# RWKV-7 recurrence and low-rank mixer on one core: 64-row products gathered, scans of 65, two raw buffers and a new order

## The chip, the cores and the metric

The kernel runs on one core of one Trainium2 chip. The metric is the device time in microseconds, the median of several runs. A profile of one further execution shows where the time goes: it has a span, from the first to the last instruction, and the execution's own time, which is a little longer.

The engines have short names: PE is TensorE (matrix products; PEld its weight loads), DVE is VectorE, ACT is ScalarE, POOL is GpSimd and SP is SyncE, which here only issues DMAs. Each engine works off its own queue in order.

## The reference

Two blocks follow each other. The first is a recurrence over 768 steps, for 4 batches and 8 heads of 40 channels. The second mixes along the sequence at rank 32 and then applies two projections with a ReLU between them.

```python
# r, k, v, w, a, b: (4, 8, 768, 40)
for t in range(S):
    y[:, :, t] = einsum('bhd,bhde->bhe', r_t, state)
    Sa = einsum('bhde,bhe->bhd', state, a_t)
    state = state * w_t[:, :, None, :] - einsum('bhd,bhe->bhde', Sa, b_t) \
            + einsum('bhd,bhe->bhde', v_t, k_t)
x = y.transpose(0, 2, 1, 3).reshape(4, 768, 320)
h = x.transpose(0, 2, 1) @ U @ V               # U (768, 32), V (32, 768)
u = x + h.transpose(0, 2, 1)
out = u + maximum(u @ w_ch1, 0) @ w_ch2        # w_ch1 (320, 1280), w_ch2 (1280, 320)
```

All inputs are made from random numbers; the six of the recurrence are float32, and the mixer's weights are 64-bit floating-point numbers in DRAM, which the kernel turns into float32 itself.

## The kernel before

**Units.** The sequence is cut into 12 chunks of 64 steps, and the batches into two pairs. A unit is one chunk of one batch pair, so there are 24 units; units 0 to 11 belong to the first pair and 12 to 23 to the second. Within a chunk the recurrence is written as products with a triangular matrix that has to be inverted; between chunks the state is carried.

**What a unit does.** Three functions write a unit's operations. `prep_f` (line 663) loads w, a, b and k, turns w over on TensorE (`wT`), and builds running products of w in both directions with two scans on VectorE: `bs` (line 686) runs backward over w in PSUM, `fs` (line 700) forward over a copy of w in SBUF that ScalarE makes (`WF`). Five blocks of 64 columns lie side by side; a one in `C1` and a zero in w at each block's border start a new product (`z`). `pl` and `rc` make the product over the whole chunk and its reciprocal. `Pn` turns the forward result over, `Q` the backward one; `KB` and `AH` (line 729) multiply k, b and a by them; the product `F` and its mask `mF` (line 789) give the triangular matrix, which goes to DRAM (`nd`) and comes back in lanes (`ln`).

`lanes` (line 794) inverts 32 x 32 triangles lane by lane, in thirty steps of two instructions each (lines 817 and 818), for all units of a group at once. Group 0 runs on VectorE, the others on POOL. Groups 0 and 1 (`F16`) take half as many steps and end with products on TensorE (`doubled`: `Ma`, `Mb`). The result goes through DRAM again (`gd`, `AB`). `prep_t` (line 845) makes the 64 x 64 inverse from the 32 x 32 ones (`XB` at line 871, then the products `T1` and `T2`). `carry` (line 904) is the serial part: `He`, `H`, `X` and `S` update the state, and `C` and `Y` give the unit's rows of y, which line 989 writes to `XTM`.

**The mixer.** `mixer` (line 1104) runs once for each batch pair, when its 12 units are done. `ph` is the product with U, `rs` adds partial sums, `V` is the product with V, and line 1140 adds it to x. Then follow six groups of two units. In each, u is turned over (`uT`, in three pieces of 128, 128 and 64 channels), ten blocks of 128 columns of w_ch1 give the hidden layer (`up`), ScalarE and VectorE apply the ReLU in turn (`hid`), and ten products per unit with w_ch2 give the result (`dn`). With 320 channels, each up block is two products on 128 rows and one on 64. Before, two blocks share a pair of PSUM banks, and the two 64-row products of the pair come last:

```python
def f(j=j, p=p):
    for y in range(2):
        mm(p.ap[:, y, 0:GN], W1[2][half(y), (j + y) * 128:(j + y + 1) * 128], ufs[2].ap[half(y)], start=False)
```

The third piece of u is needed in both halves of the partitions. Before, four ordinary products with an identity write it there.

**Weights.** `piece` (line 1031) loads a block of a weight into the raw buffer `CV` and converts it with two instructions on ScalarE and six on VectorE, with `CG` as scratch. There is one buffer of each. `weights1` brings w_ch1, U and V early, `weights2` brings w_ch2, in ten pieces.

**The order.** No line of the program says what comes when. Each operation is handed to a plan with an engine, an assumed duration, the buffers that it reads and writes, and a priority. `order` (line 185) then places them one by one: whichever engine is free takes the ready operation with the lowest priority number, if PSUM has room (three pairs of banks and two single ones). The base priority comes from the unit's number. To it is added an offset by the operation's name from the table `SHIFT` (line 1286), which has variants for early units (`0`) and those of the second pair (`*`). Where TensorE would fall idle for long, the plan puts in fillers (`idle`, line 1281): products of 512 columns in bfloat16 whose result is not read. The plan ends as a fixed order for each engine, and that order is what is compiled.

Of the kernel before, what the change touches and what calls it, by code (L numbers as in the profile page):

```python
# [53 lines left out]
class Op:  # L54
    __slots__ = ("eng", "ns", "fn", "pri", "deps", "users", "wait", "ps", "first", "mode", "start", "end", "lat",
                 "n", "left", "name", "ready", "act", "hw", "late")
# [9 lines left out]
class Pace:  # L66
# [8 lines left out]
    def worked(self, a, z, x):  # L75
        for i, w in enumerate(self.w):
            s = i * WIN / 2
            b, y, end = a + s, x, z + s
            while b < end - 1e-6:
                k = int(b // WIN + 1e-9)  # L80
                q = min(end, (k + 1) * WIN)
                if q <= b:
                    q = end
                part = y * (q - b) / (end - b)
                w[k] = w.get(k, 0.0) + part
                y -= part
                b = q
# [234 lines left out]


# [3 lines left out]
def kernel(  # L327
# [26 lines left out]
    NS = 5 * L  # L354
# [66 lines left out]
    nc.vector.memset(C1[:, L - 1:NS:L], 1.0)  # L421
# [49 lines left out]
    tRB, tQD = ring("tRB", 1, NS), ring("tQD", 1, 2 * NS)  # L471
    tFW, tD1, tWF = (ring(key, n, NS) for key, n in (("tFW", 1), ("tD1", 1), ("tWF", 1)))
# [17 lines left out]
    CG = ring("CG", 1, WP)  # L490
# [58 lines left out]
    for t in tWF:  # L549
        zeros([whole(t)], [t[:]], 320, -90.0)  # L550
# [17 lines left out]
    for t in tLT2:  # L568
        PL.add("DVE", 1700, lambda t=t: parts(t), w=[whole(t)], pri=-40.0, name="parts")
# [9 lines left out]
    PL.add("DVE", 1400, m16, w=[bM16], pri=-40.0, name="m16")  # L579
# [5 lines left out]
    GROUPS = [[0], [1, 2], [3, 4, 5], [6, 7, 8], [9, 10, 11], [12, 13, 14], [15, 16, 17], [18, 19], [20, 21], [22, 23]]  # L585
# [77 lines left out]
    def prep_f(n, pri, lane):  # L663
# [3 lines left out]
        RB, FW, D1, WF = B(tRB, n), B(tFW, n), B(tD1, n), B(tWF, n)  # L667
# [3 lines left out]
        def f():  # L671
            for x in range(2):
                tr(strided(pw.ap, [[128, 2], [1, L]], 64 * x), W.ap[:, 160 * x:160 * x + 128])
            for x in range(2):
                for y in range(2):
                    mm(pw.ap[64 * y + 32 * x:64 * y + 32 * x + 32, 256:320], W.ap[half(y), 160 * x + 128:160 * x + 160],
# [5 lines left out]
        PL.add("ACT", 435, lambda: act(WF.ap.rearrange("p (k t) -> p k t", t=L)[:, :, 1:],  # L682
                                       pw.ap[:, 0:NS].rearrange("p (k t) -> p k t", t=L)[:, :, 0:L - 1]),
               r=[pw], w=[WF], pri=pri, name=f"WF{n}")
        PL.add("DVE", 70, lambda: nc.vector.memset(pw.ap[:, 0:NS + 1:L], 0.0), r=[pw], w=[pw], pri=pri, name=f"z{n}")
# [8 lines left out]
                                       RB.ap.rearrange("p (c t) -> p c t", t=L).unsqueeze(2).to_broadcast([128, 5, 2, L])),  # L694
               r=[RB], w=[QD], pri=pri, name=f"dup{n}")
        PL.add("DVE", 175, lambda: nc.vector.tensor_tensor(out=w0.ap, in0=RB.ap[:, 0:NS:L], in1=WF.ap[:, 1:NS:L], op=ALU.mult),
               r=[RB, WF], w=[w0], pri=pri, name=f"pl{n}")
        PL.add("DVE", 190, lambda: nc.vector.reciprocal(out=D1.ap[:, 0:NS:L], in_=w0.ap),
               r=[w0], w=[D1], pri=pri, name=f"rc{n}")
        PL.add("DVE", 830, lambda: nc.vector.tensor_tensor_scan(  # L700
            out=FW.ap, data0=WF.ap, data1=D1.ap, initial=0.0,
            op0=ALU.mult, op1=ALU.add), r=[WF, D1], w=[FW], pri=pri, name=f"fs{n}")

        def f():
            for y in range(2):
                tr(pp.ap[:, y, 0:128], FW.ap[:, 128 * y:128 * y + 128])
            for y, x in QUADS:
                mm(pp.ap[half(x), y, 128:160], FW.ap[half(y), 256:320], ID[half(y), 64 * y + 32 * x:64 * y + 32 * x + 32])
        PL.add("PE", 617, f, r=[FW], w=[pp], pri=pri, mode=2, name=f"Pn{n}")
# [7 lines left out]
        def f():  # L717
# [3 lines left out]
            for x in range(2):  # L721
                for y, z in QUADS:
                    mm(pq.ap[half(z), y, 160 * x + 128:160 * x + 160], RB.ap[half(y), 256:320],
                       ID[half(y), 64 * y + 32 * x:64 * y + 32 * x + 32])
        PL.add("PE", 952, f, r=[QD, RB], w=[pq], pri=pri, mode=0, name=f"Q{n}")
        PL.add("DVE", 810, lambda: nc.vector.tensor_tensor(
            out=strided(S["KB"].ap, [[L, 2], [2 * L, NH], [1, D]]), in0=pq.ap[:, :, 0:DM].rearrange("p t (c e) -> p t c e", e=D),
            in1=KB.ap.rearrange("p (t c e) -> p t c e", t=2, e=D), op=ALU.mult), r=[pq, KB], w=[S["KB"]], pri=pri, name=f"KB{n}")
        PL.add("DVE", 500, lambda: nc.vector.tensor_tensor(
# [58 lines left out]
    def masked(o, p, m, pri, name):  # L788
        PL.add("DVE", 1200, lambda: nc.vector.tensor_tensor(  # L789
# [4 lines left out]
    def lanes(g, pri):  # L794
# [6 lines left out]
        eng, e = (nc.vector, "DVE") if g == 0 else (nc.gpsimd, "POOL")  # L801
# [9 lines left out]
        for j in range(1, top - 1):  # L811
# [7 lines left out]
            c = 450 + 3.3 * nd_ * j * m if e == "POOL" else 350 + 2.0 * nd_ * j * m  # L819
# [5 lines left out]
    def doubled(n, S, AB, DT, XB, pri):  # L825
# [10 lines left out]
        PL.add("DVE", 610, lambda p=p: nc.vector.tensor_tensor(  # L836
# [4 lines left out]
        PL.add("DVE", 610, lambda p=p: nc.vector.tensor_tensor(out=XB.ap, in0=p.ap, in1=AB.ap, op=ALU.add),  # L841
# [3 lines left out]
    def prep_t(n, lane, pri):  # L845
# [16 lines left out]
        else:  # L862
            for y in range(2):
# [7 lines left out]
            PL.add("DVE", 620, lambda: nc.vector.tensor_tensor(  # L871
                out=XB.ap.rearrange("p (h x t) -> p h x t", x=2, t=32),
                in0=AB.ap.rearrange("p (h t) -> p h t", t=32).unsqueeze(2).to_broadcast([128, NH, 2, 32]),
                in1=HB[:].unsqueeze(1).unsqueeze(3).to_broadcast([128, NH, 2, 32]), op=ALU.mult), r=[AB, bHB], w=[XB], pri=pri + 0.02,
                name=f"XB{n}")
# [28 lines left out]
    def carry(n, pri):  # L904
# [56 lines left out]
        if n + 2 < N:  # L961

            for u in range(2):
                PL.add("DVE", 380, lambda u=u: nc.vector.memset(
# [3 lines left out]
        PL.add("DVE", 1200, lambda: nc.vector.tensor_tensor(  # L968
# [27 lines left out]
    def decayed(n, pri):  # L996
# [12 lines left out]
        PL.add("DVE", 830, lambda: nc.vector.tensor_tensor(  # L1009
# [3 lines left out]
        PL.add("DVE", 500, lambda: nc.vector.tensor_tensor(  # L1013
# [17 lines left out]
    def piece(dst, dbuf, srcs, pri):  # L1031
# [7 lines left out]
        raw, g = B(CV, i), B(CG, i)  # L1039
        rb = raw.ap[:, 0:2 * n]  # L1040
# [484 lines left out]
```

## Time and profile before

| | |
|---|---|
| median of 3 runs | 765.96 us (764.36 to 768.99) |
| profiled execution, its own time | 766.89 us |
| its span | 765.1 us |
| mean granted TensorE clock | 0.956 |
| TensorE busy | 716.4 us (94%) |
| VectorE busy | 383.0 us (50%) |
| ScalarE busy | 274.4 us (36%) |
| GpSimd busy | 286.5 us (37%) |
| fillers (line 1283) | 272, busy 75.9 us |
| bytes moved by DMA | 53.51 MB, 97% of the packets under 512 B |

Busy time of an engine is the time in which one of its instructions runs. Products on TensorE are pipelined: the duration of one runs on while the next has begun, so costs are read from start to start. A float32 product shows as two records. The granted clock is 1 at full speed and 0.5 at half.

### The profile page before, as it was taken

What the parts mean: (1) busy time and instruction counts of PE and PEld (TensorE: products, weight loads), DVE (VectorE), ACT (ScalarE), POOL (GpSimd) and SP (SyncE); (2) the same over time, 40 slices, a digit from 0 to 9 for tenths busy, and PEclk for the clock granted to TensorE, in tenths of its full rate; (3) what the DMA queues carried; (4) which work ended last, traced back from release to release, by engine and by line L of the source; (5) the groups of instructions that cost most, each with busy time, mean ns of one, the idle gap of its engine ahead of it and who ended that gap; (6) DMA issues with size and microseconds to landing.
All of it is one profiled execution on the core that took longest, in us unless ns stands there. A gap on an engine that the chain in (4) does not pass through costs nothing.

```text
span 765.1 us, 27488 instructions
## 1 busy us (share of the span) xinstructions
PE 716.4 (94%) x12098; PEld 514.9 (67%) x12098; DVE 383.0 (50%) x743; ACT 274.4 (36%) x569; POOL 286.5 (37%) x551
## 2 busy tenths in 40 slices
PE   7998988897799997999989999999999999999997
PEld 4556767676677862676757777777877566767664
DVE  7685878785967777556740266641513311011110
ACT  3534545554545651154620264542432010111100
POOL 5004388965930048200087286588810000000000
PEclk8998989998889998999989999999999999999999
DMA  8766865655356462234640335521210000000001
GB/s 128 130 108 131 151 112 108 123 105 101 63 106 103 94 120 68 71 70 84 117 82 10 73 52 93 90 52 38 37 39 10 18 1 18 9 17 15 14 9 30
DMA packets 238111, 53.51 MB, mean 70 GB/s; under 512 B 230944, under 2 KB 234144, under 8 KB 237984
## 3 DMA queue, kind: packets, MB, share of 16 engines
q1 hardware_dynamic: 212640, 47.74, 33.1%
q10 hardware_dynamic: 25344, 3.94, 3.2%
q8 instruction: 97, 1.59, 0.8%
q14 instruction: 30, 0.25, 0.1%
HBM read 38.27 MB, written 13.37 MB: 68 GB/s over the span
## 4 chain that ended last, share of the span: by engine, by line
PE 67%; POOL 8%; DVE 8%; DMA 8%; ACT 4%; issue 4%; SPq 1%; ACTq 0%; DVEq 0%; POOLq 0%
PE pb L612 28%; PE pc L612 25%; PE pb L609 7%; PE pb L1283 5%; POOL tLN L818 4%; POOL tTM L817 4%; DMA tW<-in_w_dram 3%; PE pc L609 1%; DMA CV<-in_moe_w_ch_dram 1%; DMA tKB<-in_b_dram 1%; DMA tLN<-nd 1%; DMA tAB<-gd 1%; SPq L602 1%; ACT slot L605 1%; DMA tA<-in_a_dram 1%
## 5 line engine op out<-in xcount | busy, mean ns | idle before, releaser
L817 POOL TENSOR_TENSOR tTM<-tLN 64x108 f32<-64x108 f32 (+32 forms) x224 | 116.6, 520 | 205.7 <-DMA tLN<-nd 140.6
L612 PE MATMUL pb<-MX,W 128*128 128x256 f32 x720 | 160.2, 403 | 1.8 <-ACT slot L605 1.8
L612 PE MATMUL pc<-W,MX 128*128 128x320 f32 x440 | 134.2, 446 | 0.0
L612 PEld LDWEIGHTS pb<-MX,W 128*128 128x128 f32 x720 | 106.6, 189 | 38.6 <-issue 19.3
L818 POOL TENSOR_TENSOR tLN<-tLN,tTM 64x108 f32<-64x108 f32 (+32 forms) x224 | 123.6, 552 | 17.6
L612 PEld LDWEIGHTS pc<-W,MX 128*128 128x128 f32 x440 | 78.9, 189 | 39.2 <-issue 12.5
L605 ACT ACTIVATE MX<-pb 128x512 f32<-128x512 f32 (+3 forms) x45 | 25.3, 565 | 182.3 <-PE pb L612 182.2
L1283 PE MATMUL pb<-C,IDP 128*128 128x512 bf16 x262 | 72.7, 402 | 5.7 <-DVE slot L789 2.1
L1182 DVE TENSOR_SCALAR MX<-pb 128x512 f32<-128x512 f32 x24 | 16.5, 689 | 97.5 <-PE pb L612 97.5
L605 ACT ACTIVATE slot<-pb 128x160 f32<-128x160 f32 (+1 forms) x84 | 35.4, 448 | 38.2 <-PE pb L612 24.2
L1283 PEld LDWEIGHTS <-IDP 128*128 128x128 bf16 x272 | 24.0, 100 | 37.0 <-issue 16.4
L1197 DVE TENSOR_TENSOR MX<-pc,XTM 128x320 f32<-128x320 f32 x22 | 10.8, 491 | 71.6 <-PE pc L612 71.0
L968 DVE TENSOR_TENSOR tCG<-pb,MU 128x1024 f32<-128x1024 f32 x24 | 29.2, 1217 | 10.1 <-PE pb L612 9.4
L605 ACT ACTIVATE JK<-tW,WLO 128x320 bf16<-128x320 f32 x24 | 13.4, 560 | 49.4 <-DMA tW<-in_w_dram 47.1
L612 PE MATMUL pb<-tRT,tVXT 64*64 64x64 f32 x1536 | 29.9, 231 | 1.1 <-ACT tRT L605 1.0
L789 DVE TENSOR_TENSOR slot<-pb,MM 128x1024 f32<-128x1024 f32 x21 | 25.6, 1221 | 10.2 <-PE pb L612 10.1
L605 ACT ACTIVATE tVXT<-pb 128x1024 f32<-128x1024 f32 x24 | 24.6, 1024 | 15.8 <-PE pb L609 14.9
L605 ACT ACTIVATE tSB<-pb 64x320 f32<-64x320 f32 x44 | 19.0, 431 | 30.6 <-PE pb L609 24.8
L871 DVE TENSOR_TENSOR tXB<-tAB,HB 128x512 f32<-128x512 f32 x21 | 16.1, 767 | 26.8 <-DMA tAB<-gd 16.4
L612 PEld LDWEIGHTS pb<-tRT,tVXT 64*64 64x64 f32 x1536 | 26.6, 144 | 4.2 <-ACT tRT L605 1.2
L605 ACT ACTIVATE tKBT<-pb 128x1024 f32<-128x1024 f32 x24 | 24.5, 1021 | 11.6 <-PE pb L609 8.5
L612 PEld LDWEIGHTS pb<-slot,tKBT 64*64 64x64 f32 x1344 | 22.0, 135 | 9.8 <-issue 4.9
(241 smaller groups left out, 1143.0 us busy)
## 6 DMA issues: line engine op xcount, KB each, us to landing
CV<-in_moe_w_ch_dram SPq DMA_DIRECT2D x18, 320.0 KB, 3.4
nd<-slot SPq DMA_DIRECT2D x42, 128.0 KB, 2.8
tW<-in_w_dram SPq DMA_DIRECT2D x48, 80.0 KB, 3.7
tKB<-in_k_dram SPq DMA_DIRECT2D x48, 80.0 KB, 3.7
tR<-in_r_dram SPq DMA_DIRECT2D x48, 80.0 KB, 2.9
tVX<-in_v_dram SPq DMA_DIRECT2D x48, 80.0 KB, 3.3
out_dram<-MX SPq DMA_DIRECT2D x48, 80.0 KB, 2.1
tLN<-nd SPq DMA_DIRECT2D x21, 128.0 KB, 3.3
```

The source lines that it names most:

```text
L602: (eng or nc.sync).dma_start(out=o, in_=i)
L605: nc.scalar.activation(out=o, in_=i, func=kw.pop("func", ACTF.Copy), **kw)
L609: nc.tensor.matmul(out=o, lhsT=i, rhs=ident, is_transpose=True, start=True, stop=True, skip_group_check=True)
L612: nc.tensor.matmul(out=o, lhsT=l, rhs=x, start=start, stop=stop, skip_group_check=True)
L789: PL.add("DVE", 1200, lambda: nc.vector.tensor_tensor(out=o.ap.rearrange("p (s i t) -> p s i t", s=2, t=L), in0=p.ap[:].rearrange("p s (i ...
L817: eng.tensor_tensor(out=y, in0=at([[32, j], [0, m]], j), in1=at([[0, j], [1, m]], 33 * j + 1), op=ALU.mult)
L818: eng.tensor_tensor(out=at([[32, j], [1, m]], j + 1), in0=at([[32, j], [1, m]], j + 1), in1=y, op=ALU.add)
L871: PL.add("DVE", 620, lambda: nc.vector.tensor_tensor(out=XB.ap.rearrange("p (h x t) -> p h x t", x=2, t=32), in0=AB.ap.rearrange("p (h t) ...
L968: PL.add("DVE", 1200, lambda: nc.vector.tensor_tensor(out=CG.ap.rearrange("p (s t) -> p s t", t=L), in0=pc.ap[:].rearrange("p s (i t) -> p ...
L1182: PL.add("DVE", 680, lambda o3=o3, p=p: nc.vector.tensor_scalar_max(o3, p.ap[:, :, 0:GN], 0.0), r=[p], w=[hb], pri=q + 0.02, name=f"hid{pr}")
L1197: PL.add("DVE", 490, lambda p=p, n=n, ob=ob: nc.vector.tensor_tensor(out=ob.ap, in0=p.ap[:, 0:DM], in1=XTM[:, n, :], op=ALU.add), r=[p, xt ...
L1283: nc.tensor.matmul(out=t[:] if len(t.shape) == 2 else t[:, 0, :], lhsT=ib[:, 0:128], rhs=cb[:, 0:512], start=True, stop=True, skip_group_c ...
```

## The change

The parts of the change are these.

1. **64-row products of the up projection.** Four blocks now share a pair of PSUM banks, so ten blocks take three pairs. The 64-row products come first and together: in the first mixer the four, four and two of each pair of banks, in the second all ten in a row. The 128-row products follow. An eviction of the hidden layer covers two pairs of blocks instead of one.
2. **Third piece of u.** Two transposes write it to the lower half of the partitions, and two copies on VectorE bring it to both halves of SBUF. The other two pieces are both copied by ScalarE.
3. **Scans of 65.** A block is now 65 columns wide, with a border column before each 64. The zero of the backward scan and the start of the forward scan both lie there, so that both scans read w in PSUM. The copy `WF` and the product `pl` go; a small copy takes `pl`'s name. `Pn` becomes four products of 64 columns instead of two transposes.
4. **Groups and engines.** Units 0 and 1 are groups of their own, followed by groups of two to three; there are eleven groups instead of ten, and the short form `F16` covers two units instead of three. Group 0's lanes move to POOL, `AH` of units 0 to 5 moves to POOL, and `XB` moves to ScalarE as two instructions.
5. **Two raw buffers.** Weights alternate between `CV` and a part of W2's storage, until the pieces that lie there come up themselves; `CG` gets a second buffer.
6. **The order.** A base priority comes from the longest way from an operation to the end, with assumed durations and latencies. New offsets are added, with a class of its own for the units of group 2. The assumed durations of many operations are changed, and a rounding in the count of TensorE's activity is corrected.

```diff
+    def rank(self):
+        for o in self.ops[::-1]:
+            o.way = o.ns + GAP[o.eng] + max(((o.lat if u.eng != o.eng or o.eng == "SP" else 0.0) + u.way for u in o.users), default=0.0)
+            o.pri = -o.way / 15000.0
...
-    NS = 5 * L
+    NS = 5 * (L + 1)
...
-    CG = ring("CG", 1, WP)
+    CG = ring("CG", 2, WP)
...
-    GROUPS = [[0], [1, 2], [3, 4, 5], [6, 7, 8], [9, 10, 11], [12, 13, 14], [15, 16, 17], [18, 19], [20, 21], [22, 23]]
+    GROUPS = [[0], [1], [2, 3], [4, 5, 6], [7, 8, 9], [10, 11, 12], [13, 14, 15], [16, 17], [18, 19], [20, 21], [22, 23]]
+    AHP, LANV, XBA, ZXA = 6, 0, 1, 0
+    TAILS = ((0, 1, 2),)
...
-        PL.add("ACT", 435, lambda: act(WF.ap.rearrange("p (k t) -> p k t", t=L)[:, :, 1:],
-                                       pw.ap[:, 0:NS].rearrange("p (k t) -> p k t", t=L)[:, :, 0:L - 1]),
-               r=[pw], w=[WF], pri=pri, name=f"WF{n}")
...
-            out=FW.ap, data0=WF.ap, data1=D1.ap, initial=0.0,
-            op0=ALU.mult, op1=ALU.add), r=[WF, D1], w=[FW], pri=pri, name=f"fs{n}")
+            out=FW.ap, data0=pw.ap[:, 0:NS], data1=D1.ap, initial=0.0,
+            op0=ALU.mult, op1=ALU.add), r=[pw, D1], w=[FW], pri=pri, name=f"fs{n}")
...
-                tr(pp.ap[:, y, 0:128], FW.ap[:, 128 * y:128 * y + 128])
+                for x in range(2):
+                    mm(pp.ap[half(x), y, 0:128], FW.ap[:, G * (2 * y + x):G * (2 * y + x) + L], ID)
...
+        eng, e = (nc.gpsimd, "POOL") if n < AHP else (nc.vector, "DVE")
...
-        eng, e = (nc.vector, "DVE") if g == 0 else (nc.gpsimd, "POOL")
+        eng, e = (nc.vector, "DVE") if g < LANV else (nc.gpsimd, "POOL")
...
+                    PL.add("ACT", 390, lambda x=x: act(XB.ap.rearrange("p (h x t) -> p h x t", x=2, t=32)[:, :, x, :],
+                                                       AB.ap.rearrange("p (h t) -> p h t", t=32), scale=HB[:, x:x + 1]),
...
-        raw, g = B(CV, i), B(CG, i)
+        raw, g = PL.buf(W2F, 8 * DM, 8 * DM + 2 * WP) if i % 2 and dbuf not in bW2[8:] else B(CV, 0), B(CG, i)
...
+            for ks in (((0,), (1,), (2,)) if pr == 0 else TAILS):
+                js = [j for k in ks for j in quads[k]]
+                def f(js=js, dst=dst):
+                    for j in js:
+                        mm(dst(j), W1[2][half(j % 2), j * 128:(j + 1) * 128], ufs[2].ap[half(j % 2)], start=j % 4 < 2, stop=False)
...
+    PL.rank()
     for o in PL.ops:
         o.pri += SHIFT.get(kind(o.name) + o.late, 0.0)
```

## The prediction

> **What bounds the kernel now.** I read the page first, then the busy time by stage, then TensorE's order of time in the tail.
>
> ```profile
> span 765.1 us, 27488 instructions
> PE 716.4 (94%) x12098; PEld 514.9 (67%) x12098; DVE 383.0 (50%) x743; ACT 274.4 (36%) x569; POOL 286.5 (37%) x551
> PE   7998988897799997999989999999999999999997
> PEclk8998989998889998999989999999999999999999
> ```
>
> TensorE (PE) is the bound by share, but 94% is not all work: the kernel issues fillers, products of 512 columns whose result nobody reads (line 1283). So I cut the span where TensorE starts the two U products that open the two mixers (284.8 and 602.4 us by the rows of U) and asked for busy time by stage, first of everything, then of line 1283 alone (count in brackets).
>
> ```profile
> core 0: us, PE busy (x) PEld busy (x) DVE busy (x) ACT busy (x) POOL busy (x), PEclk, DMA share, GB/s
> 0.00:86.00 86.00, 74.49 (x1440) 48.52 (x1440) 61.20 (x159) 38.37 (x82) 21.44 (x63) 0.90 0.73 126
> 86.00:284.00 198.00, 174.65 (x4650) 137.35 (x4648) 148.24 (x270) 107.18 (x229) 110.83 (x200) 0.92 0.57 106
> 284.00:602.00 318.00, 309.33 (x5228) 222.30 (x5228) 149.28 (x269) 112.82 (x229) 154.22 (x289) 0.97 0.31 61
> 602.00:766.00 164.00, 157.94 (x792) 106.72 (x790) 24.28 (x47) 16.07 (x31) 0.00 (x0) 0.99 0.06 14
> ...
> 0.00:86.00 86.00, 25.05 (x94) 8.25 (x94) 0.90 0.73 126
> 86.00:284.00 198.00, 29.54 (x104) 8.63 (x104) 0.92 0.57 106
> 284.00:602.00 318.00, 17.31 (x58) 5.65 (x58) 0.97 0.31 61
> ```
>
> Stage 1 (to 284 us, the first twelve units) is held by waits: 34.9 us idle, 198 fillers, a granted clock of 0.90 to 0.92. Stage 2 (to 602 us, twelve units beside the first mixer) is TensorE's work, but for 8.7 us idle and 58 fillers. Stage 3, the second mixer alone, is TensorE without a gap, in six equal groups: the down products of one start at 675.11 and of the next at 699.69, so 24.58 us each. One group, TensorE in order of time (start, duration; a product of float32 has two records):
>
> ```profile
> 674.52 0.66 PE L612 MATMUL pc<-IDP,XTM 128*64 128x128 f32 x8
> 675.11 6.73 PE L612 MATMUL pc<-W,MX 128*128 128x320 f32 x24
> 681.67 2.52 PE L612 MATMUL pb<-MX,W 128*128 128x256 f32 x12
> 684.13 1.34 PE L612 MATMUL pc<-W,MX 128*128 128x320 f32 x4
> 685.31 2.52 PE L612 MATMUL pb<-MX,W 128*128 128x256 f32 x12
> ...
> 696.21 1.03 PE L612 MATMUL pb<-MX,W 128*128 128x256 f32 x4
> 697.07 0.38 PE L609 MATMUL pc<-IDP,XTM 128*128 128x128 f32 x2
> 697.29 1.03 PE L612 MATMUL pb<-MX,W 128*128 128x256 f32 x4
> ```
>
> Count from start to start, since durations overlap. Two full up products: 696.21 to 697.07, 0.43 us each. Twelve down products: 675.11 to 681.67, 0.547 each.
>
> **The gathered 64-row products.** The x12 row holds four full up products and one pair of 64-row ones: 681.67 to 684.13 is 2.46, less 4 x 0.43 leaves 0.74 for the pair. The two down products behind take 1.18 (684.13 to 685.31) where 2 x 0.547 is 1.09. A pair runs at once in the two halves of the rows, so its own work is 0.43; the other 0.31 + 0.09 = **0.40 us is the price of going to 64 rows and back**. A group has five pairs. The Trainium skill, "TensorEngine Tiling (Array Packing)", Key Properties, says that changing the tiling mode drains the array; that rule gives five pairs in a row one entry and exit. By row and rule a group saves 4 x 0.40 = 1.6 us; if instead each pass of 64 rows pays (no row shows two pairs together), it saves some 0.75. I take 1.6, because the U product, also on 64 rows, has 48 records from its start at 284.84 to that of the next product at 286.62: six passes of eight tiles and 320 columns, 0.30 each, where a down product's pass of 320 columns takes 0.27. Its entry and exit are paid once. The second mixer gathers all ten: 6 x 1.6 = 9.6. The first gathers 4, 4 and 2, three entries for five: 6 x 0.8 = 4.8. The gathered products hold all three pairs of PSUM banks at once; in the tail the last quad's eviction has 20 down products (10.9 us) to finish in, so I cost it at nothing.
>
> **The third transpose of u.** 674.52 to 675.11, 0.59 us for four plain products; now two transposes with 64 columns out. Two of 128 columns take 0.22 (697.07 to 697.29). The same skill page, Restrictions, speaks against it: column tiling disables transpose mode for float32, which would leave the 0.59. The gain is 0 to 0.37; I take 0.3, 12 times: 1.8 in each mixer. The second VectorE copy (0.42 us) hides behind down products.
>
> **The scans.** Line 700 takes 889 ns from SBUF, line 686 823 ns from PSUM; ScalarE loses WF (24 x 0.43), and the two pieces that replace pl stay near 0.2. The step of 65 costs TensorE: Pn's two transposes (about 0.31 to 0.37) become four 64-column products, by the row at 674.52 0.59. So +0.25, 24 times: 4.3 in stage 1, 1.8 in stage 2. pw stays in PSUM until the forward scan; the two single banks are also those of H, X, S and Y, which the new order must allow for.
>
> **Other engines.** Off VectorE in stage 1: XB (767 ns) of nine units, the three AH of units 3 to 5 and the three before them (0.6 each), the small lanes of group 0, and the doubling of unit 2: some 20 us of 209. On it: eight of the ten w_ch2 conversions now stand before the first U product (none did), some 3.2 us each. So VectorE is no lighter there, and much lighter in stage 2. POOL gains group 0's lanes, a thirty-step group of 64 rows (near 29 us) and six AH, in a stage where it was busy 132 of 284.
>
> **The order.** Every queue is reordered, so I go by what the instruction order shows. Fillers up to the first U product: 198 before, 244 after. From there to the second U product: 58 before, 5 after. Then: 16 before, 27 after. They mark where TensorE is expected to wait. Seventeen in a row at 292.28 last 3.84 us, 0.226 each; in half-clock stretches nearer 0.30.
>
> Stage 1: fillers +46 x 0.226 = +10.4; Pn +4.3; one unit less doubled -1.8; one PL group more +0.5; T1, T2 and X of one more unit already there +1.8; one wT and kT not yet -1.2. That is +14.0. Idle time was 34.9; unit 2 now waits for thirty lane steps, against which stand durations in the plan that are those of the rows (ST 640, was 500 for a row of 686; masked 1222, row 1217). I take -5.5, bounds -20 and +20. **+8.5**.
>
> Stage 2: 53 fillers less at 0.24, -12.7; gathering -4.8; transposes -1.8; Pn +1.8; units shifted -1.8 and +1.2; eight more down products of the first mixer left over, -4.3. Half the 8.7 us idle goes with the waits for w_ch2 and for u, -4.4.
>
> ```profile
> 298.00:309.00 11.00, 9.99 (x44) 0.53 0.19 60
> 387.00:394.00 7.00, 6.75 (x38) 0.53 0.59 92
> ```
>
> These two stretches (PE busy, then the clock) ran at near half clock: some 8.5 us lost. The Trainium skill, "TensorE: Matmul & The Clock Gate", says that an idle window of 3.4 us halves the clock; by it all 8.5 return where nothing idles, yet here PE was busy 91 to 96% in them. I take half, -4. **-30.8**; a new wait on w_ch2 or lanes would take the first term back.
>
> Stage 3: the eight down products +4.3; gathering -9.6; transposes -1.8; all V products now precede the first up products, each waiting for its VectorE addition (0.82), which the extra fillers mark, +2.5 for eleven. **-4.6**. A group becomes 24.58 - 1.6 - 0.3 = 22.7.
>
> Sum: -26.9 from the profiled execution's own 766.9 (its span 765.1 and 1.8 around it), **740**. The median of the runs shown is 766.0, 0.9 less, within what I can resolve; a measurement tells about 1%, so no change is 758.3 to 773.6.
>
> **Rivals.**
> - *The gain is smaller*: each 64-row pass pays (0.75 a group instead of 1.6, 0.3 instead of 0.8: 6 x 0.85 + 6 x 0.5 = +8), and half of the fillers removed from stage 2 come back as waits (+6): 754. For it: no row shows two pairs together. Against it: the U product.
> - *No change*: stage 1 lengthens by 34 instead of 8.5. For it: DMA share 0.73 at the start, K of two units is now issued ahead of the first W on SP (four issues, which took 3.76 us in the old order), and the new fillers stand in units 1, 2, 4 and 10. 765.
> - *Slower*: AH of units 3, 4 and 5 now stands in POOL's order among the lane steps of units 0 and 1. If its Pn or its A is late, the lanes behind it wait, then T1, X and every carry. Each costs up to a unit of stage 1, (284 - 86) / 11 = 18 us: 3 x 18 less the 8.5 counted, 785. It decides once the added waits pass 27 us. Against it: stage 1's POOL is idle more than half.
> - *The change does not do what it says*: the order lists four, two or ten 64-row products in a row, all scans of 65 and both raw buffers, so this gets no chance of its own.
>
> **Chances.** Forecast 0.62 (own range 726 to 755), smaller gain 0.20, no change 0.10, slower 0.08. Faster by over 1%: 0.82; within 1%: 0.10; slower: 0.08. The range runs from 718, where stage 1 sheds its bound of 20 and TensorE's whole half-clock loss of stage 2 returns, to 766, where the no-change rival ends; what is left out is the slower case and the edge of the others.
>
> **What would show it.** Right: six groups of 22.7 in the tail; the 64-row products in a row at about 0.22 a pass; fillers and idle nearly gone between the U products, which stand near 293 and 580; PEclk 9 from there on. Wrong: a group at 24 or more (gather), a first U product after 310 (stage 1, with POOL's waits for AH or tLN telling why), idle of over 10 us in stage 2.

## The result, and the profile after

The changed kernel took 742.92 us (median of 4 runs, 740.71 to 744.88); the kernel before took 765.16 us on the same chip (4 runs, 758.73 to 768.99). The ratio is **0.972, with a 95% interval of 0.964 to 0.979**: faster by 2.8%. The forecast was 740, so its sum holds to 3 us. Its stages hold less well, and most can be learned from them.

First the head of the page of the kernel after: span, busy time of the engines, and the two rows of 40 slices for TensorE and its granted clock.

```profile
span 741.5 us, 27587 instructions
PE 698.5 (94%) x12134; PEld 511.8 (69%) x12134; DVE 359.6 (49%) x688; ACT 280.2 (38%) x577; POOL 323.3 (44%) x645
PE   6889799898998898999999999999999999999997
PEclk9789999999999899999999999999999999999999
```

TensorE's share is the same 94%, now of a span that is 23.6 us shorter. VectorE has lost 23.4 us, ScalarE and POOL have gained 5.8 and 36.8. From the 17th slice on the row PE stands at 9 to the last slice but one, and the clock too; before, both rows still had an 8 in the 21st slice. So the share of busy time over the whole span does not show where the time went.

The two U products that open the mixers now start at 298.9 and 581.0 us. So the cut by stage is made at 299 and 581, and at 117, where the first rows of y are written. First everything, then the fillers alone (line 1313 now) in stage 1.

```profile
core 0: us, PE busy (x) PEld busy (x) DVE busy (x) ACT busy (x) POOL busy (x), PEclk, DMA share, GB/s
0.00:117.00 117.00, 98.51 (x1785) 62.49 (x1787) 81.99 (x185) 48.64 (x102) 69.49 (x162) 0.91 0.70 129
117.00:299.00 182.00, 165.08 (x4527) 126.18 (x4529) 132.19 (x252) 109.13 (x230) 97.37 (x179) 0.98 0.57 109
299.00:581.00 282.00, 280.15 (x5058) 210.34 (x5057) 119.56 (x207) 108.60 (x220) 156.43 (x305) 1.00 0.31 57
581.00:742.00 161.00, 154.78 (x782) 112.80 (x781) 25.90 (x48) 13.85 (x25) 0.00 (x0) 1.00 0.06 15
...
0.00:117.00 117.00, 37.99 (x125) 11.06 (x125) 0.91 0.70 129
117.00:299.00 182.00, 33.58 (x119) 9.44 (x119) 0.98 0.57 109
```

Read per stage, cut at the U products and at the ends of the span (idle time is the length of a stage less PE busy; the loss to the clock, used below, is a length times one less the granted clock):

| | stage 1 | stage 2 | stage 3 |
|---|---|---|---|
| length before, us | 284.8 | 317.6 | 162.7 |
| length after, us | 298.9 | 282.1 | 160.5 |
| difference | +14.1 | -35.5 | -2.2 |
| predicted | +8.5 | -30.8 | -4.6 |
| TensorE idle, before to after, us | 34.9 to 35.4 | 8.7 to 1.9 | 5.2 to 5.7 |
| fillers, before to after | 198 to 244 | 58 to 5 | 16 to 27 |

Stage 2 is where the time came from: TensorE has a 282 us stage with 1.9 us idle, five fillers (1.59 us busy) and a granted clock of 1.00.

In stage 3, one group in TensorE's order (start, duration, engine, line, form, count; a float32 product has two records):

```profile
629.00 0.38 PE L615 MATMUL pc<-IDP,XTM 128*64 128x128 f32 x2
629.21 1.89 PE L618 MATMUL pb<-MX,W 128*128 128x256 f32 x8
630.94 0.38 PE L615 MATMUL pc<-IDP,XTM 128*128 128x128 f32 x2
631.16 0.38 PE L615 MATMUL pb<-IDP,XTM 128*128 128x128 f32 x2
631.38 11.24 PE L618 MATMUL pc<-W,MX 128*128 128x320 f32 x40
642.55 9.53 PE L618 MATMUL pb<-MX,W 64*128 64x256 f32 x52
651.92 0.38 PE L615 MATMUL pc<-IDP,XTM 128*64 128x128 f32 x2
```

The third piece of u is the row at 629.00, two transposes, and the next row starts 0.21 us later (0.59 for four products before). The ten 64-row products stand first in the row at 642.55, with 32 records of 128 rows behind them; the pieces of u of one group and the next are 651.92 - 629.00 = **22.92 us** apart, as against 24.58 before and 22.7 predicted.

### The profile page after: what moved, and what is told of

The parts are those of the page before. It is cut to its first block, busy times and chain, and to the rows that moved or that the text cites. A ratio compares the mean times of both kernels' runs of the same rounds, so it can differ in the third digit from the quotient of the medians.

```text
span 741.5 us, 27587 instructions
## 1 busy us (share of the span) xinstructions
PE 698.5 (94%) x12134; PEld 511.8 (69%) x12134; DVE 359.6 (49%) x688; ACT 280.2 (38%) x577; POOL 323.3 (44%) x645
## 3 DMA queue, kind: packets, MB, share of 16 engines
q8 instruction: 97, 1.59, 0.9%
## 4 chain that ended last, share of the span: by engine, by line
PE 77%; DMA 9%; DVE 4%; ACT 4%; issue 3%; SPq 2%; ACTq 1%; POOL 0%; DVEq 0%; POOLq 0%
PE pb L618 40%; PE pc L618 23%; PE pb L615 8%; PE pb L1313 5%; DMA W<-in_moe_w_ch_dram 2%; SPq L608 2%; DMA CV<-in_moe_w_ch_dram 2%; PE pc L615 1%; DMA tVX<-in_v_dram 1%; DMA tW<-in_w_dram 1%; DMA tA<-in_a_dram 1%; DMA tAB<-gd 1%; DVE tCG L980 1%; DMA tR<-in_r_dram 1%; ACT slot L611 1%
## 5 line engine op out<-in xcount | busy, mean ns | idle before, releaser
L823 POOL TENSOR_TENSOR tTM<-tLN 64x84 f32<-64x84 f32 (+11 forms) x268 | 133.8, 499 | 140.8 <-DMA tLN<-nd 110.4
L824 POOL TENSOR_TENSOR tLN<-tLN,tTM 64x84 f32<-64x84 f32 (+11 forms) x268 | 139.0, 519 | 21.0
L618 PE MATMUL pb<-MX,W 64*128 64x256 f32 (+1 forms) x720 | 141.6, 388 | 0.0
L618 PEld LDWEIGHTS pb<-MX,W 64*128 64x128 f32 (+1 forms) x720 | 110.0, 188 | 29.2 <-issue 13.8
L618 PE MATMUL pc<-W,MX 128*128 128x320 f32 x400 | 124.5, 444 | 0.2
L611 ACT ACTIVATE MX<-pb 128x1024 f32<-128x1024 f32 (+4 forms) x37 | 24.7, 674 | 183.9 <-PE pb L618 182.9
L1210 DVE TENSOR_SCALAR MX<-pb 128x1024 f32<-128x1024 f32 x12 | 14.7, 1225 | 74.1 <-PE pb L618 74.1
L976 DVE MEMSET tVX<- 64x320 f32 x44 | 14.3, 325 | 34.6 <-PE pc L618 13.3
L618 PE MATMUL pb<-W,MX 128*128 128x320 f32 x80 | 29.9, 457 | 0.0
L876 DVE STREAM_TRANSPOSE tDT<-tAB 128x256 f32<-128x256 f32 x22 | 9.7, 442 | 41.3 <-DMA tAB<-gd 24.2
L611 ACT ACTIVATE tVXT<-pb 128x1024 f32<-128x1024 f32 x24 | 24.6, 1023 | 12.1 <-PE pb L615 11.9
```

The costliest lines, as they stand in the source:

```text
L611: nc.scalar.activation(out=o, in_=i, func=kw.pop("func", ACTF.Copy), **kw)
L618: nc.tensor.matmul(out=o, lhsT=l, rhs=x, start=start, stop=stop, skip_group_check=True)
L823: eng.tensor_tensor(out=y, in0=at([[32, j], [0, m]], j), in1=at([[0, j], [1, m]], 33 * j + 1), op=ALU.mult)
L824: eng.tensor_tensor(out=at([[32, j], [1, m]], j + 1), in0=at([[32, j], [1, m]], j + 1), in1=y, op=ALU.add)
L976: PL.add("DVE", 325, lambda u=u: nc.vector.memset(VX.ap[half(u), 512 * (1 - u):512 * (2 - u)].rearrange("p (c e) -> p c e", e=L)[:, :, 0:D ...
L1210: PL.add("DVE", 150 + 530 * nz, lambda o4=o4, i4=i4: nc.vector.tensor_scalar_max(o4, i4(), 0.0), r=[p], w=hbs, pri=q + 0.02, name=f"hid{pr}")
```

## The experiments

Seven kernels were compared with the kernel after and the kernel before. The kernel after ran again in one set with the first three (pairs, third piece, no fillers); the other four are a second set. In both sets the kernel before took 763 us (medians 763.52 of 13 runs and 763.09 of 19). The second set has no run of the kernel after beside it, so its kernels are judged by their ratio to the kernel before. Stage lengths are those of the profiled execution, cut at the U products as above.

In the profiles of the experiments, that without fillers apart, some 50 TensorE records are missing: fewer products than weight loads (PEld) are listed, and the difference is in the fillers. Where a count of fillers is given below, it is that of the weight loads. Idle time read from these profiles would be too long by the missing fillers (some 11 us for 50, at 0.226 each), so it is read only from the profiles before and after and from the one without fillers.

**The kernel after again.** No edit.

> The changed kernel itself, as the level for the three kernels run with it on the same chip. Every theory expects about 743 us (0.972 of before), six tail groups of 22.9 us, the first U product near 299 us and the second near 581 us.

746.15 us, ratio 0.975 (0.969 to 0.982). The stages were 303.1, 282.2 and 160.2 us, the groups 22.93. Stages 2 and 3 repeat to 0.3 us, stage 1 does not: 298.9 in one execution and 303.1 in the other, of the same kernel. With the next two kernels, which keep the order of stage 1 too, four executions had their first U product between 295.6 and 303.1, and their first rows of y between 111.7 and 117.3. In the three kernels below that are edited only in stage 1 or in fillers, stages 2 and 3 were 281.4 to 282.1 and 159.7 to 160.3. So an edit in stages 2 and 3 can be read to about 1 us from one profile, and an edit in stage 1 worth less than some 7 us cannot.

**The 64-row products in pairs again**, in the order of the kernel after. The third piece multiplied by the last pair of a group is here that of the group that follows, since its copy stands ahead in the held order; the work is of the same size.

```diff
                 def f(js=js, dst=dst):
-                    for j in js:
-                        mm(dst(j), W1[2][half(j % 2), j * 128:(j + 1) * 128], ufs[2].ap[half(j % 2)], start=j % 4 < 2, stop=False)
+                    pass
...
-                            mm(dst(j), W1[i][:, j * 128:(j + 1) * 128], ufs[i].ap, start=False, stop=i == 1)
+                            mm(dst(j), W1[i][:, j * 128:(j + 1) * 128], ufs[i].ap, start=i == 0 and j % 4 < 2, stop=False)
+                            if i == 1 and j % 2:
+                                for jj in (j - 1, j):
+                                    mm(dst(jj), W1[2][half(jj % 2), jj * 128:(jj + 1) * 128], ufs[2].ap[half(jj % 2)], start=False, stop=True)
```

> The changed kernel with its order on every engine held, but the 64-row products issued again pair by pair, each pair behind the four full products of its two blocks, in both mixers. Theory 'one entry and exit per gather' (0.40 us each, four saved per group in the second mixer, two in the first): a tail group goes from 22.9 to 24.5 us, stage 2 is 4.8 us longer, the whole is 14 us longer, about 757 us. Rival 'every pass on 64 rows pays': a tail group of about 23.7 us, the whole 8 us longer, 751 us. Rival 'the tail has slack elsewhere': no change, 743 us.

758.07 us, ratio 0.992 (0.989 to 0.996), 11.9 us above the kernel after beside it. Stage 2 took 286.5 and stage 3 169.1 us, 4.3 and 8.9 more than the kernel after beside it: +13.2 in all. That is what one entry and exit for each excursion to 64 rows makes of it (about 14), and more than the 8 by which the gain shrinks if every pass pays. Its up products, TensorE in order of time:

```profile
636.27 11.04 PE L618 MATMUL pc<-W,MX 128*128 128x320 f32 x40
647.14 10.19 PE L618 MATMUL pb<-MX,W 128*128 128x256 f32 x48
657.27 0.41 PE L615 MATMUL pc<-IDP,XTM 128*64 128x128 f32 x2
```

The row at 647.14 has 16 full products and four pairs (a row shows one of its forms). From start to start it takes 10.13 us. A full product takes 0.432 (four from 629.21 to 630.94 in the rows of the kernel after). Less twenty times 0.432, the work of 16 full products and of four pairs, 1.49 is left, or **0.37 us for each return trip** to 64 rows and back. Gathered, the same tail pays it once: its groups are 24.28 us here and 22.93 in the kernel after, so four trips fewer bring 1.35.

**The third piece of u as four products again.**

```diff
-                        tr(p.ap[0:128 if i < 2 else 64, 128 * j:128 * j + 128], x[:, 128 * i:min(128 * i + 128, DM)])
+                        if i < 2:
+                            tr(p.ap[:, 128 * j:128 * j + 128], x[:, 128 * i:128 * i + 128])
+                        else:
+                            for y in range(2):
+                                mm(p.ap[half(y), 128 * j:128 * j + 128], x[:, 256:320], ID[:])
...
-                        PL.add("DVE", 400, lambda p=p, y=y: nc.vector.tensor_copy(ufs[2].ap[half(y)], p.ap[half(0), 0:GN]), r=[p],
+                        PL.add("DVE", 400, lambda p=p, y=y: y or nc.vector.tensor_copy(ufs[2].ap, p.ap[:, 0:GN]), r=[p],
```

> The changed kernel with its order held, but the third piece of u made again by four plain products that write both halves and one copy on VectorE, instead of two transposes and two copies. Theory 'a transpose with 64 columns out costs as much as one with 128' (0.21 us for two, against 0.59): a tail group 0.38 us longer, 23.3 us, the whole 4 to 5 us longer, about 747 us. Rival 'column tiling takes the transpose mode away': no difference, 743 us.

752.68 us, ratio 0.983 (0.976 to 0.990), 6.5 us above the kernel after beside it. The group is 23.49 us: +0.56, nearly twice the 0.3 of the prediction. Stage 3 took 163.5 (+3.3), stage 2 287.7 (+5.5). TensorE in order of time:

```profile
635.73 0.38 PE L618 MATMUL pb<-MX,W 128*128 128x256 f32 x1
636.04 0.66 PE L618 MATMUL pc<-IDP,XTM 128*64 128x128 f32 x8
636.62 1.99 PE L618 MATMUL pb<-MX,W 128*128 128x256 f32 x8
638.46 0.38 PE L615 MATMUL pc<-IDP,XTM 128*128 128x128 f32 x2
```

The piece itself takes 0.58 (636.04 to 636.62) where the two transposes take 0.21: 0.37. The eight records behind it take 1.84 (636.62 to 638.46), and 1.73 behind the transposes (629.21 to 630.94): 0.11 more. The last record ahead of the piece takes 0.31 (635.73 to 636.04) instead of 0.22. So the plain products with 64 columns out, issued into both halves of the columns, pay a price at their edges as the 64-row ones do, some 0.2 us, and the transposes do not. In stage 2 the +5.5 is more than six times 0.56; what the other 2 us are was not found.

**No fillers in stages 1 and 2.** All fillers ahead of the second U product (`ph1`) are left out of the held order.

```diff
-        for o in steps:
-            o.fn()
+        cut = max(k for k, o in enumerate(steps) if o.name == "ph1")
+        for k, o in enumerate(steps):
+            if o.name != "fill" or k > cut:
+                o.fn()
```

> The changed kernel with its order held, but without the 249 fillers that stand ahead of the second U product, so that TensorE simply waits there. Theory 'fillers mark waits': nothing behind them starts earlier; the first U product is not before 297 us, TensorE's idle time in stage 1 rises by about the 56 us that the fillers took, and the granted clock falls, so the whole is the same or longer, 743 to 775 us. Rival 'fillers take TensorE's time from the work behind them': the first U product up to 30 us earlier, the whole 715 to 735 us.

742.40 us, ratio 0.971 (0.965 to 0.977): the same as with them (746.15 beside it, 742.92 in the first comparison, intervals overlapping). TensorE by stage, with the clock as the third number:

```profile
core 0: us, PE busy (x), PEclk, DMA share, GB/s
0.00:117.00 117.00, 84.38 (x1782) 0.80 0.69 129
117.00:301.00 184.00, 147.52 (x4290) 0.86 0.56 108
```

The stage still ends at 300.8, inside the spread of the same order. In the first profile of the kernel after, whose record is complete, idle time and fillers together were 107.0 us of the stage (35.4 and 71.6); here idle time alone is 69.1. The other 37.9 us went to products that ran slower: the loss to the clock is 49.2 us here and was 14.2 there (117 x 0.09 and 182 x 0.02), 35.0 more. So the fillers stand in waits that are there with or without them, and in this stage the clock that they keep up buys nothing measurable, since the slower products fill the same waits. A count of fillers is a count of waits, not a cost of its own; that is the way the prediction used it.

**The data of W ahead of that of K.** The first two `ldK` issues stand before `ldW0` on SP in the kernel after.

```diff
+        first = [o for o in steps if o.name == "ldW0"]
-        for o in steps:
+        for o in first + [o for o in steps if o.name != "ldW0"]:
             o.fn()
```

> The changed kernel with its order held, but the load of unit 0's w issued ahead of the two loads of k on SP. In the changed kernel the first product on w waits 4.1 us for that load and starts at 9.46 us; before it started at 5.81. Theory 'the late start is passed on to the end of stage 1': the first w product at about 6 us, the first U product 2 to 4 us earlier, the whole 740 us. Rival 'later waits (k's load, the lanes, T1) swallow it': the first w product earlier, the first U product unmoved within 1 us, the whole 743 us.

744.66 us, ratio 0.977 (0.969 to 0.986). The first product on W started at 5.72 instead of 9.30 and 9.46 us in the two profiles of the kernel after. The first rows of y came at 111.5 us, as against 116.5 and 117.3 there. But they came at 112.2 and 111.7 in the two kernels above with pairs and with four products, where W stands behind K and its first product starts at 9.40 and 9.63. So the earlier rows cannot be put down to W. The first U product came at 298.8 us, inside the spread of 295.6 to 303.1 of the same order. Nothing shows that the 4 us by which W is earlier reach even the first rows of y.

**AH of units 0 to 5 on VectorE again**, at its place in the order.

```diff
-        PL.add(e, 870 if e == "POOL" else 580, lambda: eng.tensor_tensor(
+        PL.add(e, 870 if e == "POOL" else 580, lambda: nc.vector.tensor_tensor(
```

> The changed kernel with its order held, but AH of units 0 to 5 done by VectorE at the same places of the order instead of POOL, where it stands among the lane steps and where the profile shows POOL waiting 8.2, 12.0, 8.4 and 3.7 us for it. Theory 'the wait of 3.7 us inside the lanes of unit 0 sets back the first carry': the first unit's rows of y 3 to 5 us earlier than 116.5 us, the first U product 0 to 4 us earlier, 739 to 743 us. Rival 'VectorE is the fuller engine there (82 of 117 us)': the same or up to 4 us later, 743 to 747 us.

745.79 us, ratio 0.976 (0.968 to 0.983): no difference from the kernel after that can be measured. POOL in the kernel after, the six AH and the first lane step (the wait and its releaser in brackets):

```profile
18.74 0.86 POOL L735 TENSOR_TENSOR tAH<-tA,slot 128x320 f32<-128x320 f32 x1 [8.23 <-issue]
31.57 1.05 POOL L735 TENSOR_TENSOR tAH<-tA,slot 128x320 f32<-128x320 f32 x1 [11.98 <-ACT slot L611]
41.07 0.86 POOL L735 TENSOR_TENSOR tAH<-tA,slot 128x320 f32<-128x320 f32 x1 [8.44 <-PE pc L618]
42.14 0.22 POOL L823 TENSOR_TENSOR tTM<-tLN 32x28 f32<-32x28 f32 x1
47.38 0.87 POOL L735 TENSOR_TENSOR tAH<-tA,slot 128x320 f32<-128x320 f32 x1 [1.06 <-DMA tA<-in_a_dram]
60.27 0.91 POOL L735 TENSOR_TENSOR tAH<-tA,slot 128x320 f32<-128x320 f32 x1 [3.67 <-PE pc L618]
69.37 0.87 POOL L735 TENSOR_TENSOR tAH<-tA,XTM 128x320 f32<-128x320 f32 x1 [1.43 <-ACT XTM L611]
```

The three long waits stand ahead of the first lane step at 42.14 us. They cost those lanes little: with AH on VectorE, POOL waits 29.07 us for the lanes' data instead and starts them at 39.95. The waits that the slower rival named, for AH of units 3, 4 and 5 among the lane steps, are the last three: 1.06, 3.67 and 1.43, 6.2 us together. With AH on VectorE they are gone, and the lanes of unit 1 end at 68.54 us, as against 70.2 to 77.5 in the six profiles with AH on POOL (the kernel after twice, and the four above). Then POOL waits 4.50 us for the data of the next group and starts it at 73.19, inside the 70.5 to 78.3 of the others. So AH does hold up the lanes of the first two units, and the wait for the next data takes that up.

**Gathering and third piece alone**, in the kernel before with its own priorities and offsets; the new operation gets the offset of the other up products. 

```diff
+    TAILS = ((0, 1, 2),)
...
-            for j in range(0, NJ, 2):
-                p = P2(side)
+            quads = [list(range(j, min(j + 4, NJ))) for j in range(0, NJ, 4)]
+            ptl = [P2(side) for _ in quads]
...
-              "zx": 0.2, "zx*": -1.1, "zx0": -0.1}
+              "zx": 0.2, "zx*": -1.1, "zx0": -0.1, "ut": -3.7, "ut*": -3.7, "ut0": -3.7}
```

> The kernel before with two parts of the change alone: the gathered 64-row products with four blocks to a pair of PSUM banks, and the third piece of u by two transposes. Its plan is made anew with the old priorities and offsets (fillers ahead of the first U product 198 as before, between the two U products 76 where before had 58 and the changed kernel 5). Theory 'the tail gains by the gather, stage 2 by the order': the first U product stays near 285 us, the tail group is 22.7 to 23 us (stage 3 shorter by 5 to 10 us), stage 2 does not get shorter than 312 us; the whole 753 to 765 us. Rival 'the mixer's parts bring most of the 22 us': 742 to 748 us.

757.68 us, ratio 0.991 (0.986 to 0.995). The stages were 284.6, 314.6 and 157.4, so -3.0 and -5.3 in the two that it touches. Two groups of the tail were 22.68, 1.9 shorter than before; two later ones, with fillers in them, 23.97 and 24.44. In stage 2 the two terms of the prediction would be worth 6.6, and 3.6 of that is missing: 76 fillers stand in it instead of 58, and 18 more at 0.226 are 4.1 us. The likely reading is that products that get shorter beside the same late data leave a longer wait; what the fillers wait for was not looked at.

**All operations of the kernel after, but the priorities, offsets and classes of the kernel before.**

```diff
-        return "*" if n >= NCH else "0" if lane[n][0] < 2 else "1" if lane[n][0] < 3 else ""
+        return "*" if n >= NCH else "0" if lane[n][0] < 2 else ""
...
-    SHIFT = {"AB": -20.7, "AB*": -24.1, "AB0": -33.6, "AB1": -11.1, "AH": 12.9, "AH*": 2.5, "AH0": 33.0, "AH1": 4.0,
+    SHIFT = {"AB": 0.4, "AB*": -3.3, "AB0": -11.5, "AH": -0.6, "AH*": -2.7, "AH0": 0.9, "AT": 2.8, "AT*": 2.9,
...
-    PL.rank()
```

> The changed kernel's operations with the priorities of before: base priority by the unit's number and the old table of offsets, no longest way. The order shows 363 fillers ahead of the first U product (244 in the changed kernel) and 24 between the two (5). Theory 'the order is what lets TensorE fill stage 2 and the operations alone do not pay': stage 1 longer by about 119 x 0.226 = 27 us, stage 2 by 4 us or more; the whole 765 to 800 us, at or above before. Rival 'the operations pay and the order is a detail': 740 to 755 us.

764.84 us, ratio 1.005 (1.002 to 1.009): **the whole gain is gone**. TensorE by stage:

```profile
core 0: us, PE busy (x), PEclk, DMA share, GB/s
0.00:92.00 92.00, 80.62 (x1559) 0.89 0.75 137
92.00:326.00 234.00, 208.63 (x5117) 0.99 0.53 102
326.00:608.00 282.00, 276.18 (x4791) 0.99 0.28 52
```

Stage 1 takes 326.4 us, 27 more than in the kernel after, with 363 fillers instead of 244; 119 more at 0.226 are 27 us. Stage 2 takes 281.9, the same as in the kernel after, where some 4 us more was expected: 4,791 records stand in it instead of 5,058, since more had been done by the first U product, while it waited. Stage 3 is 153.7, with groups of 22.68.

The offsets of the kernel before were fitted to its own operations, so this run does not say that a priority by position is worse than one by the longest way. It says that the new operations without an order of their own bring nothing. The other way round, taking the gathering and the third piece out of the kernel after costs 11.9 and 6.5 us, although both together bring only 5.4 in the kernel before (763.09 to 757.68); part of this may be that the held order was made for the shorter products. So the operations do not make the gain alone. Whether the order would is open, since the new order with the old operations was not run; the worth of the longest way without the new offsets, of the groups and of the second raw buffer was not tried by itself either.

## Why the prediction was right, step by step

**The gathered products: right in mechanism, 1.35 instead of 1.6 a group.** The return trip is 0.37 rather than 0.40, and the four that go bring 1.35. In the first mixer the pairs cost +4.3 together, predicted 4.8. The rule of the Trainium skill ("TensorEngine Tiling (Array Packing)", Key Properties), that a change of tiling mode drains the array, agrees with what was measured. The first group of the tail shows the ten gathered products by themselves:

```profile
596.64 2.43 PE L618 MATMUL pb<-MX,W 64*128 64x256 f32 x20
599.00 0.19 PE L618 MATMUL pc<-bad,ones 128*1 128x2 f32 x2
```

They take 2.36 us, 0.236 a pass. Five pairs at 0.432 are 2.16, and the 0.20 left over is less than one return trip: nothing is paid between them that can be seen.

**The third piece: 0.3 taken, 0.56 measured.** The mis-sized term is the four products. Their own time was read as 0.59 and the transposes' as 0.22, which leaves 0.37, and 0.3 was taken to allow for the same page's Restrictions, by which column tiling disables the transposes of float32. The trace after shows no sign of that with 64 columns out: 0.21 us for two. And the kernel with four products shows another 0.2 around them, which the prediction put at nothing. So the bound of 0.37 was too low: the gain lay outside "0 to 0.37".

**The scans: the cost on TensorE right, the gain on VectorE misread.** The products of `Pn` and of the fifth block behind them take 0.83 us from start to start where they took 0.56 and 0.62 in two places, +0.21 to +0.27 for the predicted +0.25. The forward scan from PSUM takes 835 ns for 325 columns (line 703). The 889 ns that it took from SBUF for 320 are a mean; half of those scans took 825 or less. So most forward scans are no shorter than before.

**Stage 1: +8.5 predicted, +14.1 measured; the idle term failed.** The 46 fillers more are there as listed. Idle time was to fall by 5.5, because the assumed durations now are those of the rows, and went from 34.9 to 35.4; why none of it went is open. The other terms alone sum to +14.0, nearly the measured length, though in a stage that varies this much that proves little. One wait at the start is longer, in TensorE's order of time (the wait and its releaser in brackets):

```profile
9.46 0.66 PE L615 MATMUL pc<-IDP,tW 128*128 128x128 f32 x2 [4.12 <-DMA tW<-in_w_dram]
```

The first product on W started at 9.46 us instead of 5.81, since W stands behind K on SP. The prediction had this queue only in its rival of no change. The kernel with W first shows no gain from it. The first rows of y came at 116.52 us instead of 86.2; what delays them by 30 us, while the stage is only 14 longer, was not looked for. The forecast put the first U product at 293.3, 2.3 us ahead of the earliest of four executions. So the miss of 5.6 is within the spread of 7.5 us but for those 2.3.

**Stage 2: -30.8 predicted, -35.5 measured; the clock term and the idle term failed, both to the good.** The loss of some 8.5 us to the clock went whole, where half was taken. The doubt came from the two stretches of the kernel before at half clock, in which TensorE was 91 to 96% busy. They have to be read with the 3.4 us ahead of each (PE busy, then the clock):

```profile
295.20:298.60 3.40, 0.92 (x5) 1.00 0.05 12
298.60:308.80 10.20, 9.79 (x43) 0.50 0.19 60
383.90:387.30 3.40, 1.61 (x18) 1.00 0.05 8
387.30:394.20 6.90, 6.65 (x40) 0.51 0.60 95
```

TensorE idled for 2.5 and 1.8 of these 3.4 us, in waits of 2.89 us for VectorE and 1.79 us for ScalarE, and the half clock came behind. In stage 2 of the kernel after the longest wait is 0.5 us, and the granted clock is 1.00. So the rule of the Trainium skill ("TensorE: Matmul & The Clock Gate", Part 1), that idle time lowers the clock, would have given all of it; here waits shorter than its idle window of 3.4 us went ahead of the half clock.

Idle fell by 6.8, predicted 4.4. The two terms together are 6.9 us better than forecast. The third piece adds to it (-5.5 by its experiment in place of -1.8), and the sum of the steps, with the measured sizes put in, then passes the measured -35.5 by some 5 us. The surplus can be narrowed down. TensorE's busy time without fillers fell by 13.1 us (308.9 less 17.3 before, 280.15 less 1.59 after). Some 5.7 of that is the clock: the 8.5 us, less half of the 5.5 us that fillers ran in the two stretches. That leaves about 7 us for the products themselves, an estimate from these figures, where the steps for the products sum to 12.9 with their measured sizes (gathering 4.3, third piece 5.5, down products 4.3, shifted units 0.6, less 1.8 for `Pn`). So the surplus is among the products, not in the waits or the clock. Which step is too large is open; some 2 us of the third piece's 5.5 had no explanation.

**Stage 3: -4.6 predicted, -2.2 measured; the end was left out.** From the trace: from the U product to the first up products 8.9 us became 15.7 (596.64 less 580.99), +6.7, with eight down products of the first mixer in it, as predicted (4.3 + 2.5). From there to the first down products of the tail 14.6 became 11.9, -2.8. From the first to the last down product 132.7 became 124.7, -8.0. These are -4.1, close to the forecast. The rest is at the end, where nothing had been counted. The last rows of the kernel after (TensorE's fillers behind the last down product, then SP's issues), and under them SP's of the kernel before:

```profile
733.20 2.75 PE L1313 MATMUL pb<-C,IDP 128*128 128x512 bf16 x12
733.38 2.99 SPq L608 DMA_DIRECT2D out_dram<-MX  x4
...
759.40 1.11 SPq L602 DMA_DIRECT2D out_dram<-MX  x2
```

Both units of the last group are now finished together, so four output issues stand behind each other on SP (2.99 us), where the kernel before had two (1.11 us), and 8.3 us pass from the last down product to the end instead of 6.4: +1.9. Also, the twenty down products of a group take 11.17 us (631.38 to 642.55), in the two kernels with the old priorities 10.97; these 0.2 are most of the difference between their groups of 22.68 and the 22.93 here. Their cause was not looked for.

**The rivals.** The smaller gain rested on a price for each 64-row pass and on fillers that come back as waits; the 2.36 us of the gathered row, and the five fillers and 1.9 us idle of stage 2, rule both out. No change rested on a longer stage 1 by 34 us; the kernel with the old priorities has one that is longer by 41.6 (326.4 against 284.8) and takes as long as the kernel before. So a stage 1 longer by that much can use up the gain, and with these operations the new order averts it. That it would come from the queue on SP, as the rival had it, is not shown: the 119 fillers more account for 27 us of it. The slower one had its waits, but 6.2 us of them where it needed more than 27, and taking them away changed the time by nothing measurable.

The prediction's misses have both signs: stage 1 by +5.6, stage 2 by -4.7, stage 3 by +2.4. That 740 came so near 742.9 owes something to that.

## What to carry to other kernels

Cut the span at landmarks that both kernels have, and count in each stage the idle time, the fillers or other padding, and the granted clock: a tuned kernel that looks 94% busy throughout can hide 58 fillers in one stage, where a better order needs five. Work that uses part of the array is best issued together, since here the price was at the edges (0.37 us a return trip) and not in the passes. But shorter work pays only where nothing late stands beside it, so an edit to the operations and an edit to their order have to be judged together. Look at the last few microseconds by themselves: two units that finish together double the issues behind the last product.

## What the runs showed of the hardware that had not been expected

- Plain float32 products into 64 columns cost some 0.2 us beyond their own 0.58, at their edges. Transposes with 64 columns out cost nothing extra: 0.21 us for two, as against 0.22 with 128.
- Taking the fillers out of stage 1 lowered the granted clock from 0.91 to 0.80 up to 117 us, and from 0.98 (0.94 in the other execution) to 0.86 from there on, and the stage did not get longer.
- In the kernel before, half clock set in behind stretches of 3.4 us in which TensorE was busy for 0.92 and 1.61, and lasted 10.2 and 6.9 us, through work that kept TensorE busy.
- A stage with DMA shares of 0.57 to 0.70 varied in length by up to 7.5 us (295.6 to 303.1) over four executions with one and the same order in it, while the stages with shares of 0.31 and 0.06 repeated to 0.3 us in two executions of one kernel. Whether the DMA is the cause was not tried.
